# A static instruction order remade from other durations, in a chunked attention with two fp32 layers behind it

## The chip, the cores and the metric

One core of a Trainium2 chip runs the whole program in one launch. The metric is the time of one execution on the device in microseconds, the median of 3 runs. The engines are PE (TensorE), DVE (VectorE), ACT (ScalarE), POOL (GpSimd) and SP (SyncE, which issues the DMAs here).

## The reference

```
attention, q, k, v of (4, 8, 576, 64), in chunks of 64 rows:
    scores = q_c @ k_c.T / 8;  attn = softmax(scores);  out = attn @ v_c
x = out as (2304, 512)
layer 1:  h = x @ w_in (512 x 2048);   g = s * relu(h)**2 + b;   y = g @ w_out (2048 x 512)
layer 2:  h = y @ w_in';               g = softplus(h);          z = g @ w_out'
```

## The kernel before

The tokens are taken as 18 tiles of 128 (two tiles make a unit, three units a group of N = 384 columns, so there are three groups j). Everything is fp32. A product of two fp32 matrices is made of three fp32r matmuls: each operand is split into a high part, which ACT writes as a cast (L505), and a low part, which DVE writes as the difference (L514); high*high, high*low and low*high are added up in PSUM.

**Attention** (tiles t = 0 to 17). For each tile: PE makes the scores (L733), DVE takes the row maximum (L747). For the first six tiles DVE scales the maximum (L769) and ACT makes eight exponentials with their sums (L757); for the others DVE subtracts (L779), ACT takes the exponential (L792) and DVE adds up (L800). DVE forms the reciprocal (L810, L811), POOL multiplies by it (L817), PE transposes (L833), ACT or DVE copies the result out of PSUM (L350 or L352), PE multiplies by the values (L852). Three PSUM buffers, named at, hold scores, transposed tiles and results in turn.

**First product of a layer.** It runs over 24 quads: a quad is 2 by 2 blocks of 128 rows of w_in for one group, made with seven products (L916) in place of eight. The forms that these need (sums and differences of quarters of x and of the weights) are made beforehand: on x by `odd_forms`, `forms`, and on the weights by `weights1`, with DVE and POOL sharing the additions (both record at L492). Inside a quad, products 6, 7 and 5 are chained through PSUM by copies on ACT (L938 and L350/L352) and by differences on DVE (L492); the finished blocks leave through ACT (L948).

**Second product.** In layer 1 six blocks of 16 steps (L1093) read the hidden features back from DRAM, square and scale them, split them and add up in four PSUM buffers. In layer 2 seven products by three groups of eight steps (L1244) do the same with sums that DVE and POOL formed. The weights arrive as 64-bit floats and are turned into fp32 by `convert` (L400 to L472, five instructions on DVE and one on ACT).

**What sets the order.** Nothing is ordered by hand. Each piece of work is recorded as an `Op` with the engines that may run it and a duration on each, a key (the due time written by its author), its dependencies and the buffers that it takes. `Work.order` then plans: again and again it takes the engine whose next piece can start first, among the pieces that can start within 0.02 us of that the one with the lowest key, and gives it its start, its end and its buffers. The list sorted by start is emitted once, so each engine's instructions stand in that order, and each engine works them off in turn: an instruction that waits holds up all behind it. The planned times are used for nothing else; what runs on the chip is the order and the choice of engine and buffer. The durations come from the small functions `dve`, `act`, `pool` and `mm`, and between two pieces on different engines the planner puts a fixed delay:

```
SAME, OTHER, LOAD = 0.13, 0.15762, 2.0
def dve(n, fast=False, pointers=0): return (144 + n / (1.6 if fast else 1)) / 960 + 0.14 * pointers
def act(n, psum=False, pointers=0): return 0.155 + n * 0.00085 + (0 if psum else 0.035) + 0.1 * pointers
def pool(n): return 0.55 + n * 0.0015
```

Of the kernel before, what the change touches and what calls it, by code (L numbers as in the profile page):

```python
# [21 lines left out]
DM = H * D  # L22
DFF = 2048
KK = DM // P
# [9 lines left out]
N = GROUP * P  # L34
# [62 lines left out]

class Work:
# [6 lines left out]
    SAME, OTHER, LOAD = 0.13, 0.15762, 2.0  # L105
# [24 lines left out]
    def order(self, places):  # L130
        free = {k: {i: 0.0 for i in range(n)} for k, n in places.items()}
        engine = {"PE": 0.0, "ACT": 0.0, "DVE": 0.0, "SP": 0.0, "POOL": 0.0}
        memory = 0.0
# [25 lines left out]
        while len(done) < len(self.ops):  # L159
# [10 lines left out]
            t, op, e = best  # L170
# [9 lines left out]
            engine[e] = t + cost  # L180
            op.end = t + cost
# [3 lines left out]
            for u in op.gives:  # L185
                u.left -= 1
                u.until = max(getattr(u, "until", 0.0), op.end)
                if u.left == 0:
                    free[u.kind][u.index] = u.until + self.OTHER
# [26 lines left out]
def block_attention_two_layers(  # L216
# [271 lines left out]
    def sub(key, out, x, y, n, deps, uses=(), op=None, e="DVE", **kw):  # L488
        return add(
            {e: pool(n) if e == "POOL" else dve(n)},  # L490
            key,
            lambda e: on(e).tensor_tensor(  # L492
                out=out(), in0=x(), in1=y(), op=op or ALU.subtract
            ),
            deps,
            uses,
            **kw,
        )

    def split(key, hi, lo, x, n, deps, uses=(), psum=False, r=(), wh=(), wl=()):  # L500
# [11 lines left out]
            {"DVE": dve(n)},  # L512
# [98 lines left out]
    def odd_forms(ph, u, even, odd, key, deps, uses):  # L611
# [18 lines left out]
        o1 = sub(key, x(0), lo(odd), lo(even), 256, deps, uses, after=turn.get("T", ()))  # L630
# [62 lines left out]
    def attention(t, key):  # L693
# [34 lines left out]
        def scores(e):  # L728
# [16 lines left out]
            {"DVE": dve(DM)},  # L745
# [29 lines left out]
        else:  # L775
            o3 = add(
                {"DVE": dve(DM)},
# [20 lines left out]
                {"DVE": dve(DM)},  # L798
# [9 lines left out]
        def reciprocals(e):  # L808
# [6 lines left out]
            {"POOL": pool(DM)},  # L815
# [14 lines left out]
        def turned(e):  # L830
# [7 lines left out]
            {"ACT": act(DM, True), "DVE": dve(DM)},  # L838
# [21 lines left out]
        if hold or not odd:  # L860
            xo = Place("xo")
            c = add(
                {"ACT": act(DM, True), "DVE": dve(DM)},
                key,
                lambda e: copy(e, at(xo), at(px)),
                [o10],
                [px, xo],
            )
            held[t] = xo, c
# [25 lines left out]
    def quad(ph, i, j, w, keys, kinds):  # L895
# [66 lines left out]
        def kept(n, go, o, key):  # L962
# [8 lines left out]
            {"ACT": act(N, True), "DVE": dve(N)},  # L971
# [7 lines left out]
        d7 = sub(keys[5] - 1, lambda: at(dd), acc(ba), lambda: at(s2), N, [p7], [ba, s2, dd])  # L979
        p5 = product(5, ba, [sc, d7])  # L980
        sd = sub(keys[3] - 1, acc(bd), acc(ba), lambda: at(dd), N, [p5], [ba, dd, bd])
# [28 lines left out]
    def block(ph, j, half, t0, first):  # L1010
# [3 lines left out]
        accs = [Place(x) for x in kinds]  # L1014
        gl = None
        for m in range(NM):
# [69 lines left out]
            for d in range(4):  # L1086

                def go(e, d=d, m=m, hi=hi, lo=lo, w2=w2):
# [19 lines left out]
                )  # L1108
                if m == NM - 1:
# [3 lines left out]
                        {"ACT": act(N, True), "DVE": dve(N)},  # L1113
# [28 lines left out]
    def second_by_blocks(ph, t0):  # L1142
# [69 lines left out]
        for z, (n, j) in enumerate(steps):  # L1212
            accs = [Place(x) for x in (("S", "at"), ("S", "at"), ("S", "at"), ("A", "A"))[z % 4]]
            wp, apart = v2[n]
            for i in range(NF):
# [21 lines left out]
                def go(e, i=i, hi=hi, lo=lo, wp=wp, apart=apart, accs=accs):  # L1237
# [18 lines left out]
                    [*parts, *v2_ready[n, i]],  # L1256
# [14 lines left out]
            for d in range(2):  # L1271
                for y, (to, of) in enumerate(plan):
                    dst = (ysum[j] + (to * 2 + d) * N, N)
                    ps = lambda d=d, accs=accs: at(accs[d])[:, :N]
                    if of is None:
                        f = add(
                            {"ACT": act(N, True), "DVE": dve(N)},
# [6 lines left out]
                    else:  # L1284
# [9 lines left out]
                            ALU.add,  # L1294
                            r=[src],
# [177 lines left out]
```

## Time and profile before

| | |
|---|---|
| median of 3 runs | 832.77 us (832.23 to 833.54) |
| span of the profiled execution | 834.3 us |
| PE busy | 795.1 us (95%) |
| weight loads on PE | 775.0 us (93%) |
| DVE busy | 654.0 us (78%) |
| ACT busy | 506.4 us (61%) |
| POOL busy | 148.6 us (18%) |
| mean granted TensorE clock | 0.992 |

The profiled execution is one execution; its span is 1.5 us above the median of the timed runs. PE's idle time is not spread evenly: the slices of the span show it in the first eighth, around 480 us and at the very end. A busy PE is not PE at its peak, since a slow clock and waits inside a row of matmuls count as busy too, so the number of matmuls in a window says more than its busy share.

### The profile page before, as it was taken

The page shows a single profiled execution, that of the slowest core. Times are in us where ns is not written, and L with a number is a line of the kernel's source. Part 1 is how long each engine was busy: PE and PEld are TensorE (multiplying, and loading weights), DVE is VectorE, ACT ScalarE, POOL GpSimd, SP SyncE. Part 2 cuts the span into 40 slices and gives each one's busy share as a digit, 9 for nine tenths or more (in the row PEclk, how much of TensorE's full clock was granted, in tenths as well). Part 3 has the DMA queues.
Part 4 walks back from the last instruction along what each step waited for, and adds up shares of the span by engine and source line. Part 5 has one row for each costly group of instructions (what it writes and reads, how often), then busy time and mean ns, then how long its engine had stood idle before and what let it go on. Part 6 is the DMA issues. An engine that isn't in the chain of part 4 may idle for free.

```text
span 834.3 us, 14524 instructions
## 1 busy us (share of the span) xinstructions
PE 795.1 (95%) x5117; PEld 775.0 (93%) x5117; DVE 654.0 (78%) x1174; ACT 506.4 (61%) x1076; POOL 148.6 (18%) x162
## 2 busy tenths in 40 slices
PE   4688889999999999999999989999999999999998
PEld 3577789999998999999999989999999999999997
DVE  5799888888967869888888776778784767777865
ACT  3655555666656877767767655555555655555543
POOL 4254240111111003222213540111110000000000
PEclk9899999999999999999999999999999999999999
DMA  8665347868757835767662027657667996688851
GB/s 235 195 190 170 106 144 241 262 240 269 257 218 275 324 107 161 244 225 255 224 197 88 11 95 262 232 197 251 246 233 253 354 372 226 203 262 297 277 187 57
DMA packets 80632, 180.26 MB, mean 216 GB/s; under 512 B 9008, under 2 KB 53040, under 8 KB 79664
## 3 DMA queue, kind: packets, MB, share of 16 engines
q1 hardware_dynamic: 80560, 179.34, 63.9%
q8 instruction: 40, 0.66, 0.3%
q14 instruction: 32, 0.26, 0.1%
HBM read 111.15 MB, written 68.16 MB: 215 GB/s over the span
## 4 chain that ended last, share of the span: by engine, by line
PE 83%; DVE 8%; DMA 3%; ACT 3%; issue 1%; POOL 1%; SPq 0%; ACTq 0%; DVEq 0%
PE at L916 17%; PE S L916 10%; PE S L1093 9%; PE at L1093 9%; PE S L1244 8%; PE at L1244 8%; PE A L916 7%; PE A L1093 6%; PE A L1244 5%; DVE operands L514 2%; DVE mem L492 2%; PE at L852 2%; PE at L733 1%; DMA mem<-in_w_dram 1%; DMA last<-in_k_dram 1%
## 5 line engine op out<-in xcount | busy, mean ns | idle before, releaser
L492 POOL TENSOR_TENSOR mem<-mem 128x256 f32<-128x256 f32 x120 | 109.6, 923 | 414.1 <-DVE mem L472 309.2
L514 DVE TENSOR_TENSOR operands<-mem,operands 128x384 fp32r<-128x384 f32 (+4 forms) x186 | 130.9, 720 | 45.0 <-ACT operands L505 43.1
L505 ACT CAST operands<-mem 128x384 fp32r<-128x384 f32 (+4 forms) x186 | 112.3, 620 | 58.8 <-PE at L1244 36.1
L514 DVE TENSOR_TENSOR operands<-last,operands 128x384 fp32r<-128x384 f32 (+2 forms) x184 | 110.5, 616 | 42.4 <-ACT operands L505 39.9
L505 ACT CAST operands<-last 128x384 fp32r<-128x384 f32 (+2 forms) x184 | 94.3, 528 | 73.2 <-PE A L1093 46.5
L916 PE MATMUL at<-operands 128*128 128x384 f32 x624 | 122.4, 340 | 4.1 <-ACT mem L350 2.0
L916 PEld LDWEIGHTS at<-operands 128*128 128x128 f32 x624 | 110.4, 190 | 6.7 <-ACT mem L350 2.7
L1093 PE MATMUL S<-operands 128*128 128x384 f32 x432 | 90.7, 335 | 0.4 <-DVE operands L514 0.4
L1093 PE MATMUL at<-operands 128*128 128x384 f32 x432 | 90.3, 334 | 0.0
L1244 PE MATMUL S<-operands 128*128 128x384 f32 x384 | 87.4, 334 | 0.1
L1244 PE MATMUL at<-operands 128*128 128x384 f32 x384 | 87.1, 334 | 0.0
L916 PE MATMUL S<-operands 128*128 128x384 f32 x420 | 83.5, 337 | 0.9 <-DVE S L492 0.8
L1093 PEld LDWEIGHTS S<-operands 128*128 128x128 f32 x432 | 76.2, 188 | 0.9 <-DVE operands L514 0.6
L1093 PEld LDWEIGHTS at<-operands 128*128 128x128 f32 x432 | 76.2, 188 | 0.0
L948 ACT ACTIVATE mem<-S 128x384 f32<-128x384 f32 x104 | 50.6, 492 | 41.1 <-PE S L916 34.4
L916 PEld LDWEIGHTS S<-operands 128*128 128x128 f32 x420 | 73.5, 188 | 1.5 <-DVE S L492 1.3
L1244 PEld LDWEIGHTS S<-operands 128*128 128x128 f32 x384 | 68.3, 188 | 0.4 <-DVE operands L514 0.4
L1244 PEld LDWEIGHTS at<-operands 128*128 128x128 f32 x384 | 68.3, 188 | 0.0
L916 PE MATMUL at<-last,operands 128*128 128x384 f32 x336 | 67.2, 337 | 0.6 <-ACT S L938 0.2
L492 DVE TENSOR_TENSOR mem<-mem 128x384 f32<-128x384 f32 (+1 forms) x108 | 60.7, 589 | 9.1 <-ACT mem L948 7.8
L1093 PE MATMUL A<-operands 128*128 128x384 f32 x288 | 65.4, 334 | 0.0
L916 PE MATMUL A<-operands 128*128 128x384 f32 x300 | 60.5, 341 | 3.3 <-ACT S L938 1.5
(79 smaller groups left out, 1217.0 us busy)
## 6 DMA issues: line engine op xcount, KB each, us to landing
mem<-in_w_dram SPq DMA_DIRECT2D x64, 512.0 KB, 4.4
summed<-mem SPq DMA_DIRECT2D x168, 192.0 KB, 2.3
mem<-summed SPq DMA_DIRECT2D x30, 768.0 KB, 4.8
hid<-mem SPq DMA_DIRECT2D x96, 192.0 KB, 2.9
last<-hid SPq DMA_DIRECT2D x24, 768.0 KB, 5.3
last<-summed SPq DMA_DIRECT2D x12, 768.0 KB, 4.9
mem<-forms SPq DMA_DIRECT2D x7, 1024.0 KB, 7.1
last<-in_q_dram SPq DMA_DIRECT2D x18, 256.0 KB, 4.2
```

What stands on the lines that cost most here:

```text
L492: lambda e: on(e).tensor_tensor(out=out(), in0=x(), in1=y(), op=op or ALU.subtract),
L505: lambda e: nc.scalar.copy(out=hi().bitcast(F32R), in_=x()),
L514: lambda e: nc.vector.tensor_tensor(out=lo().bitcast(F32R), in0=x(), in1=hi(), op=ALU.subtract),
L733: nc.tensor.matmul(out_[c * D : (c + 1) * D, pr], of("q")[:, pr * P + c * D : pr * P + (c + 1) * D], kb[:, :, pr, c, :], start=True, stop= ...
L852: nc.tensor.matmul(at(px)[y, x], of("v")[y, x], of("aT")[y, x], start=True, stop=True)
L916: nc.tensor.matmul(acc(dst)().rearrange("p (u c) -> p u c", u=GROUP), l[a], r[c], start=start and kk == 0 and x == 0, stop=kk == 1 and x == 2,
L948: lambda e: nc.scalar.activation(out=at(go), in_=acc(place)(), func=AF.Softplus if ph else AF.Relu),
L1093: nc.tensor.matmul(at(accs[d])[:, :N], l[a], r[c], start=m == 0 and z == 0, stop=m == NM - 1 and z == 2,)
L1244: nc.tensor.matmul(at(accs[d])[:, :N], l[a], r[c], start=i == 0 and y == 0, stop=i == NF - 1 and y == 2,)
```

## The change

Only the planner's numbers change, and with them the order, the choice between ACT and DVE for some copies, and the PSUM buffers. No operation is added or removed: the same 3777 pieces are recorded with the same keys.

1. The delay between dependent pieces depends on the engine that ends (`AFTER`) and the one that begins (`BEFORE`), and now also holds on the same engine, other than PE.
2. DVE, ACT and POOL get other durations. On DVE a piece of n elements now takes 0.068 + n/960 us in place of 0.15 + n/960, on POOL 256 elements take 0.683 us in place of 0.934.
3. A duration can be a `Port`: pieces of DVE and POOL that are marked so may not overlap in the plan. DVE pieces that read PSUM, and sums along a row, are not marked.
4. In the blocks and in layer 2's second product each step now depends on the step before it, so that the plan can't exchange them.

```diff
+class Port(float):
+    pass
...
-    SAME, OTHER, LOAD = 0.13, 0.15762, 2.0
+    AFTER = {"PE": 0.225, "ACT": 0.133, "DVE": 0.116, "POOL": 0.078, "SP": 0.0}
+    BEFORE = {"PE": 0.02, "ACT": 0.0, "DVE": 0.0, "POOL": 0.12, "SP": 0.1}
+    HELD = {"DVE": 0.06, "POOL": 0.1}
+    LOAD = 2.0
...
         def earliest(op, e):
-            t = engine[e]
+            t = max(engine[e], port) if isinstance(op.engines[e], Port) else engine[e]
             for d in op.deps:
-                t = max(t, d.end + (self.OTHER if d.on != e else 0 if e == "PE" else self.SAME))
+                t = max(t, d.end + (self.AFTER[d.on] + self.BEFORE[e] if d.on != e or e != "PE" else 0))
...
             engine[e] = t + cost
+            if isinstance(op.engines[e], Port):
+                port = t + cost - self.HELD[e]
...
-def dve(n, fast=False, pointers=0):
-    return (144 + n / (1.6 if fast else 1)) / 960 + 0.14 * pointers
+def dve(n, fast=False, pointers=0, port=True):
+    t = 0.068 + n / 960 / (1.94 if fast else 1) + 0.058 * pointers
+    return Port(t) if port else t
 def act(n, psum=False, pointers=0):
-    return 0.155 + n * 0.00085 + (0 if psum else 0.035) + 0.1 * pointers
+    return 0.09 + n * 0.00083 - (0.035 if psum else 0) + 0.095 * pointers
-def pool(n):
-    return 0.55 + n * 0.0015
+def pool(n, spread=False):
+    return Port(0.135 + n * (0.0017 if spread else 0.00214))
...
-                    [*parts, *w2_done[ph, m]],
+                    [*parts, *w2_done[ph, m], *before[d]],
...
-                    [*parts, *v2_ready[n, i]],
+                    [*parts, *v2_ready[n, i], *([o] if i else [])],
```

**What stands where.** In the new program the line numbers of the old one are higher by 10 up to the quads (L733 is L743, L505 is L515) and by 13 at the end. On PE, about a fifth of the 942 pieces stand at another place; on DVE and ACT nearly all do, most by a few places. 74 pieces change between ACT and DVE: DVE has 1150 pieces in place of 1154, ACT 988 in place of 984. POOL keeps its 150, SP its 547.

The first place is PE at the start of the attention. In the names, at_70, at_71 and at_72 are the three PSUM buffers, and last_120 holds the tiles' inputs. Scores (L733) are of tiles 3, 4, 5 and 6 in turn, transposed tiles (L833) and values (L852) of tiles 1, 2 and 3. Before:

```order
L733 MATMUL at_71<-last_120 64x128 x8
L733 MATMUL at_70<-last_120 64x128 x8
L833 MATMUL at_72<-ident,last_120 128x128 x4
L852 MATMUL at_72<-last_120 64x64 x16
L833 MATMUL at_71<-ident,last_120 128x128 x4
L852 MATMUL at_71<-last_120 64x64 x16
L733 MATMUL at_72<-last_120 64x128 x8
L733 MATMUL at_70<-last_120 64x128 x8
L833 MATMUL at_71<-ident,last_120 128x128 x4
L852 MATMUL at_71<-last_120 64x64 x16
```

Now, from the same place on:

```order
L743 MATMUL at_71<-last_120 64x128 x8
L843 MATMUL at_70<-ident,last_120 128x128 x4
L862 MATMUL at_70<-last_120 64x64 x16
L743 MATMUL at_72<-last_120 64x128 x8
L843 MATMUL at_71<-ident,last_120 128x128 x4
L743 MATMUL at_70<-last_120 64x128 x8
L862 MATMUL at_71<-last_120 64x64 x16
L843 MATMUL at_72<-ident,last_120 128x128 x4
L743 MATMUL at_71<-last_120 64x128 x8
L862 MATMUL at_72<-last_120 64x64 x16
```

Tile 1 is transposed ahead of tile 4's scores, and tile 3 ahead of tile 6's scores and into at_72, which tile 4's scores held, where before it went into at_71, which the result of tile 2 held.

The second place is DVE at the same time: from the copy of the transposed tile 2 (L352, into last_120) to the copy of tile 3. L400, L430 and L444 turn the second weights into fp32; L514 with operands<-at_71 is the split of tile 2's result, which sets its PSUM buffer free. Before:

```order
L352 COPY last_120<-at_71 128x512
L810 TENSOR_SCALAR sm_83<-sm_83 128x8
...
L400 TENSOR_SCALAR mem<-mem 128x512
L430 TENSOR_SCALAR mem<-mem 128x512
L352 COPY mem<-at_71 128x512
...
L747 TENSOR_REDUCE mx_78<-at_72 128x8
L514 TENSOR_TENSOR operands<-mem,operands 128x1024
L514 TENSOR_TENSOR operands<-at_71,operands 128x512
L769 TENSOR_SCALAR mx_78<-mx_78 128x8
L747 TENSOR_REDUCE mx_80<-at_70 128x8
L352 COPY last_120<-at_71 128x512
```

Now, from the same weights on:

```order
L410 TENSOR_SCALAR mem<-mem 128x512
L440 TENSOR_SCALAR mem<-mem 128x512
...
L820 TENSOR_SCALAR sm_83<-sm_83 128x8
...
L362 COPY last_120<-at_71 128x512
L757 TENSOR_REDUCE mx_78<-at_70 128x8
L524 TENSOR_TENSOR operands<-mem,operands 128x1024
L362 COPY mem<-at_71 128x512
L779 TENSOR_SCALAR mx_78<-mx_78 128x8
...
L454 SCALAR_TENSOR_TENSOR mem<-mem 128x512
L524 TENSOR_TENSOR operands<-at_71,operands 128x512
L362 COPY last_120<-at_72 128x512
```

The weights' first instruction now stands ahead of the copy of tile 2 and of tile 3's reciprocal; the maximum of tile 6 no longer stands ahead of the copy of tile 3. On SP the two loads of these weights (in_w_dram) now stand ahead of the three loads of tile 7's q and k, and behind those of tile 6; before they stood behind tile 7's.

The third place is ACT early in layer 2, some 490 us into the span. L505 with last<-mem and 512 elements is a split of the forms of group 2; the first of them in each list needs no sum of POOL's, the second does. L350 is the copy that product 7 of a quad of group 1 waits for. Before:

```order
L505 CAST last_4635<-mem 128x512
L938 COPY S_68<-at_72 128x384
L948 ACTIVATE mem<-S_67 128x384
L948 ACTIVATE mem<-at_71 128x384
L505 CAST last_4635<-mem 128x512
L948 ACTIVATE mem<-S_69 128x384
L350 COPY mem<-at_72 128x384
L938 COPY S_67<-at_70 128x384
L505 CAST last_4635<-mem 128x512
```

Now:

```order
L948 COPY S_69<-at_71 128x384
L515 CAST last_4644<-mem 128x512
L958 ACTIVATE mem<-S_68 128x384
L948 COPY S_67<-at_70 128x384
L360 COPY mem<-at_71 128x384
L515 CAST last_4644<-mem 128x512
L958 ACTIVATE mem<-A_66 128x384
```

In the new list the copy stands ahead of the split that needs POOL's sum; before it stood behind it.

## Rows read from the trace of the kernel before

**Rows 1.** The page: span, busy time by engine, PE's busy tenths in 40 slices.

```profile
span 834.3 us, 14524 instructions
PE 795.1 (95%) x5117; PEld 775.0 (93%) x5117; DVE 654.0 (78%) x1174; ACT 506.4 (61%) x1076; POOL 148.6 (18%) x162
...
PE   4688889999999999999999989999999999999998
```

**Rows 2.** Busy time by window: stretch, length, engines (instructions), granted clock, DMA.

```profile
0.00:20.00 20.00, 9.47 (x57) 7.01 (x57) 11.73 (x22) 8.05 (x36) 8.36 (x17) 1.00 0.88 236
20.00:40.00 20.00, 12.84 (x172) 10.91 (x172) 13.81 (x30) 11.89 (x60) 5.61 (x6) 0.88 0.67 205
40.00:60.00 20.00, 17.04 (x268) 14.36 (x267) 18.23 (x38) 11.86 (x30) 9.44 (x10) 0.86 0.61 182
60.00:80.00 20.00, 17.44 (x270) 15.26 (x271) 19.50 (x39) 12.12 (x21) 7.99 (x10) 1.00 0.61 187
80.00:100.00 20.00, 17.51 (x252) 15.23 (x248) 17.10 (x32) 9.89 (x19) 8.31 (x8) 1.00 0.21 71
...
700.00:750.00 50.00, 50.00 (x291) 50.00 (x290) 37.90 (x71) 28.82 (x57) 0.00 (x0) 1.00 0.72 243
```

**Rows 3.** Timeline of PE, 12 to 47: start, duration, line, [idle before <-releaser].

```profile
32.57 1.15 PE L852 MATMUL at<-last 64*64 64x64 f32 x32 [1.27 <-DVE last L352]
...
39.15 1.09 PE L833 MATMUL at<-ident,last 128*128 128x128 f32 x4 [3.53 <-DVE mx L769]
41.02 1.97 PE L852 MATMUL at<-last 64*64 64x64 f32 x32 [0.78 <-DVE last L352]
```

**Rows 4.** Timeline of ACT, 15 to 47.

```profile
15.80 0.83 ACT L505 CAST operands<-mem 128x768 fp32r<-128x768 f32 x1 [3.87 <-DVE mem L472]
16.54 0.31 ACT L757 ACTIVATE last<-at,mx 128x64 f32<-128x64 f32 x1
```

**Rows 5.** Timeline of DVE, 22 to 47.

```profile
33.81 1.03 DVE L400 TENSOR_SCALAR mem<-mem 128x512 uint32<-128x512 uint32 x1 [0.47 <-DMA mem<-in_w_dram]
...
38.32 0.68 DVE L514 TENSOR_TENSOR operands<-at,operands 128x512 fp32r<-128x512 f32 x1
38.92 0.15 DVE L769 TENSOR_SCALAR mx<-mx 128x8 f32<-128x8 f32 x1
...
45.79 0.69 DVE L747 TENSOR_REDUCE mx<-at 128x8 f32<-128x512 f32 x1 [0.32 <-PE at L733]
```

**Rows 6.** The chain that ended last, 24 to 47: start, duration, what.

```profile
25.67 0.45 SPq L367
...
27.36 6.43 DMA mem<-in_w_dram
```

**Rows 7.** Timeline of DVE, 258 to 272.

```profile
265.76 0.56 DVE L492 TENSOR_TENSOR mem<-at,mem 128x384 f32<-128x384 f32 x1 [0.44 <-PE at L916]
```

**Rows 8.** Timeline of PE, 262 to 273.

```profile
266.93 1.32 PE L916 MATMUL at<-operands 128*128 128x384 f32 x6 [1.20 <-ACT S L938]
```

**Rows 9.** Timeline of PE, 484 to 498.

```profile
488.74 1.20 PE L916 MATMUL S<-operands 128*128 128x384 f32 x6
491.90 3.71 PE L916 MATMUL at<-operands 128*128 128x384 f32 x12 [1.96 <-ACT mem L350]
```

**Rows 10.** Timeline of ACT, 484 to 498.

```profile
490.47 0.62 ACT L505 CAST last<-mem 128x512 fp32r<-128x512 f32 x1 [2.56 <-POOL mem L492]
...
491.38 0.47 ACT L350 COPY mem<-at 128x384 f32<-128x384 f32 x1
```

**Rows 11.** Timeline of POOL, 470 to 497.

```profile
486.23 4.21 POOL L492 TENSOR_TENSOR mem<-mem 128x256 f32<-128x256 f32 x2 [5.38 <-ACT last L505]
...
494.64 1.43 POOL L492 TENSOR_TENSOR mem<-mem 128x256 f32<-128x256 f32 x2 [0.42 <-DVE mem L492]
```

**Rows 12.** Timeline of PE, 672 to 682.

```profile
679.83 0.44 PE L1244 MATMUL A<-operands 128*128 128x384 f32 x1 [0.46 <-ACT operands L505]
680.49 1.83 PE L1244 MATMUL A<-operands 128*128 128x384 f32 x9 [0.21 <-DVE operands L514]
```

More of the change, by code (lines that the diff above doesn't have):

```diff
@@ L132, in order @@
         engine = {"PE": 0.0, "ACT": 0.0, "DVE": 0.0, "SP": 0.0, "POOL": 0.0}
-        memory = 0.0
+        memory = port = 0.0
         users, waits = {}, {}
@@ L186, in order @@
                 u.left -= 1
-                u.until = max(getattr(u, "until", 0.0), op.end)
+                u.until = max(getattr(u, "until", 0.0), op.end + self.AFTER[e])
                 if u.left == 0:
-                    free[u.kind][u.index] = u.until + self.OTHER
+                    free[u.kind][u.index] = u.until
             done.append(op)
@@ L486, in on, with sub @@
         return nc.gpsimd if e == "POOL" else nc.vector
-    def sub(key, out, x, y, n, deps, uses=(), op=None, e="DVE", **kw):
+    def sub(key, out, x, y, n, deps, uses=(), op=None, e="DVE", port=True, **kw):
         return add(
-            {e: pool(n) if e == "POOL" else dve(n)},
+            {e: pool(n) if e == "POOL" else dve(n, port=port)},
             key,
@@ L511, in split @@
         o2 = add(
-            {"DVE": dve(n)},
+            {"DVE": dve(n, port=not psum)},
             key,
@@ L629, in odd_forms @@
         uses = [*uses, t]
-        o1 = sub(key, x(0), lo(odd), lo(even), 256, deps, uses, after=turn.get("T", ()))
+        o1 = sub(key, x(0), lo(odd), lo(even), 256, deps, uses, after=turn.get("T", ()), port=False)
         turn["T"] = [o1]
@@ L744, in attention @@
         o2 = add(
-            {"DVE": dve(DM)},
+            {"DVE": dve(DM, port=False)},
             key,
@@ L776, in attention @@
             o3 = add(
-                {"DVE": dve(DM)},
+                {"DVE": dve(DM, port=False)},
                 key,
@@ L797, in attention @@
             o5 = add(
-                {"DVE": dve(DM)},
+                {"DVE": dve(DM, port=False)},
                 key,
@@ L814, in attention @@
         o7 = add(
-            {"POOL": pool(DM)},
+            {"POOL": pool(DM, True)},
             key,
@@ L837, in attention @@
         o9 = add(
-            {"ACT": act(DM, True), "DVE": dve(DM)},
+            {"ACT": act(DM, True), "DVE": dve(DM, port=False)},
             key,
@@ L862, in attention @@
             c = add(
-                {"ACT": act(DM, True), "DVE": dve(DM)},
+                {"ACT": act(DM, True), "DVE": dve(DM, port=False)},
                 key,
@@ L970, in quad @@
         c2 = add(
-            {"ACT": act(N, True), "DVE": dve(N)},
+            {"ACT": act(N, True), "DVE": dve(N, port=False)},
             keys[7] - 1,
@@ L978, in quad @@
         sc = seed(bc, keys[5] - 1, [p7])
-        d7 = sub(keys[5] - 1, lambda: at(dd), acc(ba), lambda: at(s2), N, [p7], [ba, s2, dd])
+        d7 = sub(keys[5] - 1, lambda: at(dd), acc(ba), lambda: at(s2), N, [p7], [ba, s2, dd], port=False)
         p5 = product(5, ba, [sc, d7])
-        sd = sub(keys[3] - 1, acc(bd), acc(ba), lambda: at(dd), N, [p5], [ba, dd, bd])
+        sd = sub(keys[3] - 1, acc(bd), acc(ba), lambda: at(dd), N, [p5], [ba, dd, bd], port=False)
         b22 = hidden(ba, 1, 1, keys[5] + 1, [p5])
@@ L1014, in block @@
         accs = [Place(x) for x in kinds]
+        before = [[] for d in range(KK)]
         gl = None
@@ L1108, in block @@
                 )
+                before[d] = [o]
                 if m == NM - 1:
@@ L1112, in block @@
                     f = add(
-                        {"ACT": act(N, True), "DVE": dve(N)},
+                        {"ACT": act(N, True), "DVE": dve(N, port=False)},
                         key + dt,
@@ L1276, in second_by_blocks @@
                         f = add(
-                            {"ACT": act(N, True), "DVE": dve(N)},
+                            {"ACT": act(N, True), "DVE": dve(N, port=False)},
                             t,
@@ L1294, in second_by_blocks @@
                             ALU.add,
+                            port=False,
                             r=[src],
```

## The prediction, made before the changed kernel was timed

> **What bounds the kernel now.** Read the page first: PE is busy for 795.1 of 834.3 us, and its tenths are below 8 only in the first two slices [rows 1]. Next, the busy time by window [rows 2]. In a stretch without waits, 700 to 750, PE ends 291 matmuls in 50.00 us, 0.172 us each. The second and first products are 24 x 7 x 6 matmuls per layer, 6 x 16 x 4 x 3 and 21 x 8 x 6 of them, 4176 in all, so 718 us at that rate; no order of the same work goes below this plus the attention's own matmuls. The rest, 116 us, holds those and PE's waits, and only the waits can be won. In the first 100 us PE is busy for 9.47 + 12.84 + 17.04 + 17.44 + 17.51 = 74.3 us, so it waits for 25.7 and, at a granted clock of 0.88 and 0.86 between 20 and 60, works part of the rest at the lower of its two levels. DVE in the same windows goes from 11.73 and 13.81 to 18.23, 19.50 and 17.10: up to 40 us DVE waits too, from 40 on it is full, with 60 - 54.8 = 5.2 us to spare. So the attention has two halves: a start in which every engine waits for another (a latency bound), and a main part that DVE bounds. After 100 the waits are small and show in the tenths as one 8 around 480 [rows 1]. Last, the timelines around the larger gaps of PE, to see which wait ends last there [rows 3 to 12].
>
> **The change part by part.** The recorded pieces are the same; what moves is order, engine and buffer. Chaining the accumulations adds no instruction, and on PE, which takes its work in turn, no wait: nothing. Of the 74 pieces that change engine, DVE loses 4 net, some 0.55 us each, 2 us of 654 spread over the span: nothing on the path by itself.
>
> *The start, -3.0 us.* Three links move. First, tile 1's exponentials start at 16.54 behind a cast that began at 15.80 [rows 4]; in the new list they stand ahead of it, 0.7 us earlier, and tile 1's reciprocal and copy move forward with them. Second, the second weights: SP issues their load at 27.36, after three loads for tile 7 that begin at 25.67, and it lands 6.43 us later [rows 6]; DVE stands before it, and its conversion runs at 33.81 [rows 5]. Now the load is issued 27.36 - 25.67 = 1.7 us earlier, so it lands by 32.1, earlier if tile 7's bytes were what slowed it. Third, PE transposes tile 3 at 39.15 after 3.53 us without work [rows 3]: it waits for a PSUM buffer that DVE's split of tile 2's result sets free, at 38.32 + 0.68 [rows 5]. In the new list it takes the buffer of tile 4's scores, free once ACT has made tile 4's exponentials, which need nothing of tile 2's result. What then binds is DVE's copy of tile 3. Between the copies of tiles 2 and 3 stand, in the new list, one difference 1024 wide, four instructions 512 wide and three small ones. One of 512 takes 0.68 us, and the next starts 0.60 after it [rows 5]; with twice that for 1024 and 0.4 for the small ones, 4.0 us. The copy of tile 2 ended just ahead of its reader, 32.57 [rows 3], and stands now about where it stood, so from 33 the 4.0 us give 37.0. Before, the copy ended just ahead of its reader at 41.02 [rows 3] and so began near 40.3: 3.3 us earlier. Following the two lists on to the maximum of tile 7, the same place in both (45.79 [rows 5]), the lead stays about 3. From there DVE is full; to the end of the attention its work in the two lists differs by under 1 us, so a lead at 45 is a lead at 95, and PE's later work starts that much sooner. Bounds: 0 if the lead is used up, -4.8 if the lower clock [rows 2] also ends sooner; on the other side +1.7, since the weights' first instruction on DVE now stands ahead of tile 2's copy, and if the load lands as late as before, the earlier issue turns into that much waiting of DVE. I take -3.0, near the copy's 3.3.
>
> *The end of layer 1's first product, -1.0 us.* Product 5 of the last quad starts at 266.93 after 1.20 us [rows 8]; it waits for DVE's difference at 265.76 [rows 7], which stood behind the splits of layer 2's first weights. These splits now stand several places further ahead, and PE has product 2 between 7 and 5. What is late next: the first block's low part, five DVE instructions behind the last quad's, as before. Bounds -1.4 and +0.6.
>
> *The second layer's entry, -2.4 us.* PE ends product 6 at 488.74 + 1.20 = 489.94 and starts product 7 at 491.90, 1.96 us later [rows 9], waiting for a copy that ACT makes at 491.38, behind a cast that waited 2.56 us for POOL and ran at 490.47 [rows 10]. In the new list the copy stands ahead of that cast, and PE has another quad's product 3 in between: the 1.96 go. The twelve matmuls from 491.90 took 3.71 where 12 x 0.172 plus the last one's tail of 0.16 make 2.2 [rows 9]; a third of these 1.5 us should go too, as ACT is no longer late. POOL's pair of sums at 486.23 takes 4.21 us against 1.43 for an equal pair at 494.64 [rows 11]: DVE has instructions without a pause beside it. The new list has one DVE instruction fewer there, which wins 0.5 for POOL; since nothing urgent waits behind it now, I count nothing. Bounds -3.6 and +1.0 (a POOL sum that becomes the wait of PE itself).
>
> The Trainium skill, page "SBUF — State Buffer", section "SBUF: two separate sides", says that the pair of ports is locked for one whole instruction, by whichever of the two engines starts first. By that rule the pair at 486.23 would have waited for one DVE instruction, 0.68 us, and taken 0.68 + 1.43 = 2.1 us; the trace shows 4.21, so here a waiting POOL is passed over by several DVE instructions, and the plan, which gives POOL the port after one, is too kind to it. By the rule this entry could win the whole 3.5 us, in place of the 2.4.
>
> *The start of layer 2's second product, -0.9 us.* At 679.83 and 680.49 PE waits 0.46 and 0.21 us [rows 12], each time behind the 0.16 that the last matmul takes over its 0.172, so 1.0 in all, at the change to the A buffers, because ACT and DVE make their copies of a finished result before the splits that PE needs next. In the new lists the splits stand first. Bounds -1.1 and +0.5.
>
> *Everything else, +1.0 us.* Elsewhere after 100 us PE's gaps are small ones, behind seeds and differences inside the quads. The new order has others. That it is planned with durations nearer to the rows (0.60 us from one 512 wide DVE instruction to the next, where the old plan had 0.68 [rows 5]) speaks for fewer; that the due times are as they were, and POOL slower than planned, for more. Bounds -1.5 and +4. I take +1.0, the size of one gap such as that of [rows 8].
>
> Sum: -3.0 - 1.0 - 2.4 - 0.9 + 1.0 = -6.3. The profiled execution goes from 834.3 to 828.0. The median before, 832.77, lies 1.5 us under that span; taken off alike, the forecast is 826.5 us.
>
> **The rivals.**
>
> *POOL is starved in the attention (slower).* The lead makes DVE run without a pause earlier, and the softmax multiplication (L817) on POOL is on every tile's chain. Against 1.43, the pair of [rows 11] took 2.8 us more. For it: DVE has 19.50 of 20 us between 60 and 80 [rows 2]. Against it: in that window POOL already works 7.99 us beside that DVE, and once DVE has nothing left but what waits for POOL, POOL gets its turn. From three such multiplications on the path on, the sum turns: 3 x 2.8 = 8.4 against 6.3, so +2.1, or 834.9.
>
> *Only the transitions are won.* The lead at 45 is eaten in the main part, since PE's order there is fixed too and a tile that stands ahead of one that is ready makes it wait; ten waits of half a DVE instruction (0.3 us) are the 3.0. For it: the main part has little room to catch up [rows 2]; against it: both lists are full there. -6.3 + 3.0 = -3.3, or 829.5.
>
> *The change does not do what it says.* The order is better in the plan, but each engine's queue on the chip waits at other places, and new gaps take back what the named ones give: everything else at +4, the lead at half, -1.5, the entry at -1.5, the other two as they are, -1.9, in all -0.9, or 831.9. That is within 0.2% (1.7 us), about what a measurement of this kernel can tell from no change. For it: the due times are those of the old durations; against it: the named gaps rest on one instruction's place each.
>
> *All of it and more.* The lead with the clock, -4.8, the entry at -3.6, the other two at -2.0 and nothing new: -10.4, or 822.4.
>
> **How the numbers follow.** The forecast has 0.45, the larger gain 0.14, the transitions alone 0.17, no change 0.10, starved POOL 0.14. Faster by over 0.2%: 0.45 + 0.14 + 0.17, and a little of the neighbours' spread, 0.77; within 0.2%: 0.10; slower: 0.13. The forecast's own range is 824 to 829.2. The range that should hold 8 in 10 goes down to 821.5, below the larger gain, and up to 833.0, past no change, and leaves out starved POOL and the far ends.
>
> **What would show it.** In the changed profile, tile 3 is transposed (L843) by about 36 and not 39, with little idle before it; the second weights' load lands by 32; the maximum of tile 7 runs at about 43; DVE is no less full from 40 to 95. The gaps of PE at 266.93, 491.90 and 679.83, each some us earlier now, are under 0.4. It is wrong if L817 takes longer in the mean than before; if DVE has more idle time between 45 and 95 than the 5 us now; or if PE has new gaps of over 1 us between 100 and 660.

## The result, and the profile after

| | before | after |
|---|---|---|
| median | 832.96 us (832.23 to 833.54, 4 runs) | 818.35 us (816.57 to 819.81, 4 runs) |
| ratio of the medians, 95% interval | | 0.9825 (0.9804 to 0.9846) |
| span of the profiled execution | 834.3 us | 816.4 us |

The change makes the kernel 14.6 us faster by the medians. The prediction had the direction; its 826.5 us and its lower end of 821.5 us were too high. The two profiled spans differ by 17.9 us: the execution of before that was profiled was slower than its timed runs (span 834.3, where their median less the 1.8 us around the span that the later runs show, as 818.22 us for the span of 816.4, makes 831.2).

The page after, answering to [rows 1]:

```profile
span 816.4 us, 14526 instructions
...
PE 788.6 (97%) x5117; PEld 771.9 (95%) x5117; DVE 637.4 (78%) x1170; ACT 507.4 (62%) x1080; POOL 144.7 (18%) x162
...
PE   5788999999999999999999999999999999999998
```

PE reaches 9 tenths in the fifth slice, before in the seventh, and the 8 around 480 us is gone. DVE is busy for 16.6 us less with four instructions less: the reader should stop there, since four instructions of 0.55 us are only 2.2.

The windows, answering to [rows 2] (same columns):

```profile
20.00:40.00 20.00, 14.17 (x190) 11.66 (x188) 14.89 (x35) 14.00 (x72) 6.04 (x7) 0.74 0.67 195
40.00:60.00 20.00, 17.21 (x278) 14.86 (x275) 19.55 (x39) 11.42 (x19) 8.21 (x10) 1.00 0.72 200
...
80.00:100.00 20.00, 19.50 (x244) 17.91 (x243) 17.31 (x33) 16.14 (x32) 10.25 (x10) 1.00 0.37 123
...
700.00:750.00 50.00, 50.00 (x291) 50.00 (x290) 36.98 (x71) 28.26 (x56) 0.00 (x0) 1.00 0.77 253
```

The stretch without waits is as before, 291 matmuls in 50 us. From 80 to 100 PE is busy for 19.50 us where it was 17.51. From 40 to 60 its granted clock is 1.00 where it was 0.86, but from 20 to 40 it is 0.74 where it was 0.88; over the first 50 us the mean is 0.90 in both.

At the start, PE, DVE and the chain, answering to [rows 3, 5, 6]:

```profile
32.23 1.11 PE L843 MATMUL at<-ident,last 128*128 128x128 f32 x4
34.63 1.98 PE L743 MATMUL at<-last 128*64 128x128 f32 x16 [1.29 <-DVE operands L524]
...
36.54 1.59 PE L862 MATMUL at<-last 64*64 64x64 f32 x32
```

```profile
28.30 0.43 DVE L410 TENSOR_SCALAR mem<-mem 128x512 uint32<-128x512 uint32 x1 [0.98 <-DMA mem<-in_w_dram]
...
40.50 0.68 DVE L757 TENSOR_REDUCE mx<-at 128x8 f32<-128x512 f32 x1
```

```profile
21.78 6.50 DMA mem<-in_w_dram
```

Tile 3 is transposed at 32.23 without a wait (before 39.15, after 3.53 us of waiting), the weights land at 28.3 (before 33.8), tile 3's values start at 36.54 (before 41.02), and tile 7's maximum runs at 40.50 (before 45.79).

Around the end of layer 1's first product, the second layer's entry and the start of the last product, PE, answering to [rows 8, 9, 12]:

```profile
252.64 1.20 PE L926 MATMUL S<-operands 128*128 128x384 f32 x6
...
258.30 0.45 PE L1104 MATMUL S<-operands 128*128 128x384 f32 x1 [0.85 <-ACT operands L515]
259.06 1.14 PE L1104 MATMUL S<-operands 128*128 128x384 f32 x5 [0.31 <-DVE operands L524]
...
466.47 1.32 PE L926 MATMUL S<-operands 128*128 128x384 f32 x6 [1.39 <-ACT S L948]
...
478.24 1.20 PE L926 MATMUL at<-operands 128*128 128x384 f32 x6
...
662.58 3.63 PE L1256 MATMUL A<-operands 128*128 128x384 f32 x20
```

The 1.20 us ahead of product 5 and the 1.96 ahead of product 7 are gone (478.24 is that product 7), and the change to the A buffers has no gap. The first block now waits 0.85 and 0.31, and the entry has one new gap of 1.39. PE of before ahead of the gap of [rows 8] and at the first block:

```profile
264.52 1.21 PE L916 MATMUL at<-operands 128*128 128x384 f32 x6
...
271.05 1.15 PE L1093 MATMUL S<-operands 128*128 128x384 f32 x5 [0.38 <-DVE operands L514]
```

Where the time came from is read from the same matmul at six places of PE's list. The third column is from the first experiment, a second execution of before's order:

| PE starts | before, us | same order again, us | after, us | after's lead grows by, against the two |
|---|---|---|---|---|
| scores of tile 7 | 43.96 | 43.66 | 38.64 | 5.3 / 5.0 |
| product 7 of quad (2, 0), layer 1 | 139.80 | 140.66 | 129.22 | 5.3 / 6.4 |
| a step of the first block | 280.37 | 281.19 | 268.36 | 1.4 / 1.4 |
| a product after layer 2's entry | 520.56 | 518.80 | 505.18 | 3.4 / 0.8 |
| a step of the last product | 699.15 | 697.31 | 681.30 | 2.5 / 2.4 |
| the last matmuls | 829.15 | 827.31 | 811.30 | 0.0 / 0.0 |

The second line is the surprise: 5 to 6 us between 40 and 140 us, where the prediction had a kept lead.

### The profile page after: what moved, and what is told of

Its sections match the earlier page's. It is cut to its first block, busy times and chain, and to the rows that moved or that the text cites. A ratio compares the mean times of both kernels' runs of the same rounds, so it can differ in the third digit from the quotient of the medians.

```text
span 816.4 us, 14526 instructions
## 1 busy us (share of the span) xinstructions
PE 788.6 (97%) x5117; PEld 771.9 (95%) x5117; DVE 637.4 (78%) x1170; ACT 507.4 (62%) x1080; POOL 144.7 (18%) x162
## 4 chain that ended last, share of the span: by engine, by line
PE 88%; DVE 5%; ACT 2%; DMA 2%; issue 1%; SPq 1%; POOL 0%; DVEq 0%; ACTq 0%; POOLq 0%
PE at L926 19%; PE S L926 12%; PE S L1104 9%; PE at L1104 9%; PE S L1256 8%; PE at L1256 8%; PE A L926 8%; PE A L1104 6%; PE A L1256 5%; PE at L862 1%; DVE operands L524 1%; SPq L377 1%; PE at L743 1%; DVE mem L502 1%; DMA last<-in_k_dram 1%
## 5 line engine op out<-in xcount | busy, mean ns | idle before, releaser
L524 DVE TENSOR_TENSOR operands<-mem,operands 128x384 fp32r<-128x384 f32 (+4 forms) x186 | 126.0, 698 | 53.9 <-ACT operands L515 52.2
L515 ACT CAST operands<-mem 128x384 fp32r<-128x384 f32 (+4 forms) x186 | 111.2, 620 | 59.2 <-PE at L1256 36.2
L515 ACT CAST operands<-last 128x384 fp32r<-128x384 f32 (+2 forms) x184 | 94.4, 527 | 75.7 <-PE A L1104 48.7
```

Of the source, the lines that this page charges most:

```text
L515: lambda e: nc.scalar.copy(out=hi().bitcast(F32R), in_=x()),
L524: lambda e: nc.vector.tensor_tensor(out=lo().bitcast(F32R), in0=x(), in1=hi(), op=ALU.subtract),
```

## The experiments

A ratio is to runs of before from the same set, and need not be the quotient of the medians printed here. Before's median was 832.69 us in the sets of the first four experiments, of POOL's price and of the first moved model, 833.03 where one part is left out, and 833.66 for the last four.

**The same order once more.** Part 4 of the change alone:

```diff
-                    [*parts, *w2_done[ph, m]],
+                    [*parts, *w2_done[ph, m], *before[d]],
```

> The kernel before with part 4 of the change alone: each step of an accumulation depends on the step before it. The planned order of every engine comes out as before, piece by piece, so every theory expects 833.0 us and no difference. The run has a second use. The trace of before shows the first keys landing 1.0 to 1.7 us later than that of after, at places that the change doesn't touch, and its span is some 3 us over what its timed runs imply. If the profiled execution of before had a late start by chance, this profile has a span near 831 and tile 1's scores start at about 11.5 and not 12.46; if the late landing belongs to the order of before, they start at 12.46 again.

Measured: 833.76 us, ratio 1.0005 (0.9976 to 1.0034). Chaining makes no difference that shows. The span is 832.4; tile 1's scores start at 13.82, 1.4 us later than in before, so the landing of the first loads varies by itself; yet tile 7's scores start 0.3 us earlier. The second layer's entry came out otherwise than in before. Of this execution, POOL, DVE and PE, answering to [rows 11] and [rows 9]:

```profile
487.04 2.07 POOL L492 TENSOR_TENSOR mem<-mem 128x256 f32<-128x256 f32 x2 [5.38 <-ACT last L505]
```

```profile
487.29 1.23 DVE L514 TENSOR_TENSOR last<-mem,last 128x512 fp32r<-128x512 f32 x1
488.44 1.09 DVE L492 TENSOR_TENSOR mem<-mem 128x384 f32<-128x384 f32 x1
```

```profile
490.59 2.36 PE L916 MATMUL at<-operands 128*128 128x384 f32 x12
```

DVE of before at the same two instructions:

```profile
486.47 0.68 DVE L514 TENSOR_TENSOR last<-mem,last 128x512 fp32r<-128x512 f32 x1
487.07 0.55 DVE L492 TENSOR_TENSOR mem<-mem 128x384 f32<-128x384 f32 x1
```

In before the pair of sums took 4.21 us while DVE ran on undisturbed; here, in the same order, POOL got in, the pair took 2.07, DVE paid with 1.23 and 1.09, and product 7 has no wait ahead of it and takes 2.36 in place of 3.71. So 2.6 us of the entry in before was the outcome of one execution.

**Where the time is won.** Three kernels plan with the new numbers only in one part of the plan's own time (45 us: `now < 45`; 130 us: `now < 130`; the complement: `now >= 130`):

```diff
+            new = now < 45
...
+            if not new:
+                cost = getattr(cost, "old", None) or cost
```

> The new numbers (durations, delays and port) while the plan's own time is under 45 us, the old numbers from there on. Theory A (the gain of 14.6 us is won in three or four separate places: about 3 at the start to 45 us, 5 between 85 and 111 us where the first quads of layer 1 meet the last tiles of the attention, 3.4 at the second layer's entry, 1.6 at its second product, 1 to 2 elsewhere): 829 to 830 us, that is the start alone. Theory B (it is nearly all an earlier start, which is passed on, and the later gaps only close because everything comes sooner): 820 to 822.

> The new numbers while the plan's own time is under 130 us, so in the whole attention and in the first quads, the old numbers from there on. Theory A (separate places): the start and the handover are won, the second layer's entry and second product are not: 833 - 3 - 5 = 825 us. Theory B (an earlier start passed on): 820 to 822, and no less than the run with 45 us.

> The old numbers while the plan's own time is under 130 us, the new numbers from there on: the complement of the run before. Theory A: 14.6 - 8 = 6 to 7 us are won after the attention, 826 to 827 us. Theory B: nothing to win there beyond 1 or 2 us, 831 to 832.

Measured: up to 45, 827.15 us, ratio 0.9939 (0.9912 to 0.9966); up to 130, 823.85, 0.9901 (0.9870 to 0.9931); from 130 on, 829.53, 0.9962 (0.9940 to 0.9984). Theory B is out: its 820 to 822 us for the first two came out in neither. Theory A, separate places, holds in kind: 8.8 and 3.2 us make 12.0 of the 14.6. Its sizes hold only for the second kernel (825 expected); the first won 2 to 3 us more than its 829 to 830, and the third 3 us less than its 826 to 827, so 2.6 us belong to neither half, no more than the intervals can hide. In the trace of the first one a lead of 2.8 us at tile 7's scores (41.12 for 43.96) has shrunk to 1.0 at the product 7 that before starts at 139.80: a lead is not kept by itself. That execution took 831.33 us, 4.2 over the kernel's median, so the loss need not be as large in the others.

**Which part wins it.** The changed kernel without one part each, without the port (part 3), with the old delays (part 1), with the old durations (part 2):

```diff
-            t = max(engine[e], port) if isinstance(op.engines[e], Port) else engine[e]
+            t = max(engine[e], port) if False else engine[e]
```

```diff
-                t = max(t, d.end + (self.AFTER[d.on] + self.BEFORE[e] if d.on != e or e != "PE" else 0))
+                t = max(t, d.end + (0.15762 if d.on != e else 0 if e == "PE" else 0.13))
```

```diff
-    return Port(0.135 + n * (0.0017 if spread else 0.00214))
+    return Port(0.55 + n * 0.0015)
...
-    t = 0.068 + n / 960 / (1.94 if fast else 1) + 0.058 * pointers
+    t = (144 + n / (1.6 if fast else 1)) / 960 + 0.14 * pointers
```

> The changed kernel without its part 3: pieces of DVE and POOL may overlap in the plan, everything else new. The runs so far won 5.5 us with the new numbers up to 45 us of the plan, 8.8 up to 130 and 3.2 from 130 on, 14.6 in all, and the traces show DVE taking 3 us less for the same conversions of the first weights between 45 and 90, because fewer of them run beside an instruction of POOL. Theory P (what counts is that the plan keeps DVE and POOL apart, so that DVE's instructions are not stretched): most of the 14.6 goes, 826 to 830 us, and L444's conversions beside POOL take 1.3 to 1.6 again and not 0.68. Theory D (what counts are the shorter durations, which put each piece nearer to where the chip has it): 818 to 821 us.

> The changed kernel without its part 1: the old delays between pieces (0.13 on the same engine, 0.158 to another), new durations and port. Theory P (port): 818 to 821 us. Theory D (durations): 818 to 821. Theory W (the delays count, since DVE's and POOL's results reach another engine sooner than the old plan thought and PE's later, 0.116 + 0.02 and 0.245 in place of 0.158): 825 to 829.

> The changed kernel without its part 2: the old durations of DVE, ACT and POOL, with the new delays and the port. With the long durations the port costs the plan far more than the chip. Theory P: 820 to 824 us. Theory D: 828 to 834, the same as before or slower, since a plan that thinks POOL's pieces take 0.93 and holds DVE back for them makes DVE the bound where it is not.

Measured: without the port 842.40 us, ratio 1.0130 (1.0101 to 1.0159), slower than before; with the old delays 829.57, 0.9959 (0.9938 to 0.9980); with the old durations 835.39, 1.0035 (1.0014 to 1.0055). The port was expected to cost at most 12 and cost 24. One place of many in that trace, a block of layer 1 with a weights' conversion, all engines:

```profile
406.31 2.74 POOL L502 TENSOR_TENSOR mem<-mem 128x256 f32<-128x256 f32 x3 [2.82 <-DVE mem L482]
406.62 0.96 DVE L410 TENSOR_SCALAR mem<-mem 128x512 uint32<-128x512 uint32 x1
...
407.50 0.96 DVE L440 TENSOR_SCALAR mem<-mem 128x512 uint32<-128x512 uint32 x1
...
408.49 1.11 DVE L454 SCALAR_TENSOR_TENSOR mem<-mem 128x512 f32<-128x512 uint32 x1
...
409.53 0.55 DVE L524 TENSOR_TENSOR operands<-last,operands 128x384 fp32r<-128x384 f32 x1
...
410.13 1.16 PE L1104 MATMUL S<-operands 128*128 128x384 f32 x5 [0.99 <-DVE operands L524]
```

Three conversions beside POOL's sums take 0.96, 0.96 and 1.11; the split behind them comes late and PE waits 0.99 us. In the blocks of the changed kernel PE has no such wait (its lead is 12.01 us at 280 and at 467 alike), and its conversions on DVE stand clear of POOL:

```profile
394.42 0.68 DVE L454 SCALAR_TENSOR_TENSOR mem<-mem 128x512 f32<-128x512 uint32 x1
...
395.42 0.69 DVE L482 SCALAR_TENSOR_TENSOR mem<-mem 128x512 f32<-128x512 f32 x1
```

The kernel with old durations still has 6.4 us of lead at 268, as theory P wants, and loses 4.7 of it where PE turns to the first block (its wait there is 3.27 us); its time as a whole lies just above theory D's range.

**POOL's price by itself.** Three orders, as they are, with POOL's instructions made small:

```diff
-                out=out(), in0=x(), in1=y(), op=op or ALU.subtract
+                out=less(e, out()), in0=less(e, x()), in1=less(e, y()), op=op or ALU.subtract
...
-                out=heads(of("e")),
+                out=heads(of("e"))[:, :, :4],
```

> The kernel before with its order as it is, but each instruction of POOL made small: the sums take 16 of 256 columns, the softmax multiplication 4 of 64 per head (the rest of those values is left out; two fills of the buffers concerned stand on DVE before the first scores). POOL then occupies nothing for long. Theory P (the order of before loses its time where DVE and POOL meet): 818 to 823 us, near the changed kernel's 818.35. Theory O (it loses it because pieces stand in the wrong places, whatever they take): 829 to 833.

> The order that was planned without the port (842.4 us), with POOL's instructions made small in the same way. Theory P: the plan without the port is right about a chip on which POOL takes nothing from DVE, so the time falls to 812 to 820 us, by more than 22. Theory O: 835 to 840.

> The changed kernel with POOL's instructions made small in the same way. Theory P: its order already keeps the two engines apart, so little is left to win: 813 to 817 us. Theory O: the same 2 to 5 us as the other two.

Measured, and what POOL costs each order (the medians' difference to the same order with POOL's full work; ratios are to before):

| order | POOL full | POOL small, ratio | POOL costs |
|---|---|---|---|
| before | 832.69 us | 822.50 us, 0.9889 (0.9824 to 0.9953) | 10.2 us |
| planned without the port | 842.40 us | 823.86 us, 0.9885 (0.9828 to 0.9942) | 18.5 us |
| after | 818.35 us | 817.04 us, 0.9814 (0.9762 to 0.9867) | 1.3 us |

The full and the small kernel of the last two orders were timed in different sets; by the ratios POOL costs 9.2, 20.4 and 0.9 us, so the last is not told from nothing. Theory P holds in direction for all three and in size for the first; the last, at 817.04, lies at the edge of its 813 to 817, and the middle one fell by 18.5 and not by over 22. Theory O's 829 to 833 and 835 to 840 came out in neither of the first two. But POOL's price is not all: with POOL small in both, the order after is still 5.5 us faster than the order before (817.04 against 822.50). POOL's price thus explains 8 to 9 of the 14.6 us, and other places the rest. The trace of before with POOL small shows which: read at the same matmuls it leads before by 2.0 us at tile 7's scores, 7.5 at product 7 of layer 1, 12.8 behind layer 2's entry and 13.3 at the end, where the changed kernel leads by 5.3, 10.6, 15.4 and 17.9. From 44 to 140 both win some 5.4; 3.3 us of the start and 2 of the last product are not had by making POOL small.

One rival is left in these runs. A small POOL instruction also ends sooner itself (a sum takes 0.34 us in the mean and not 0.92), so what "POOL costs" holds waits for POOL's results as well as DVE's lengthened work, and no run separates the two. In the traces ACT's waits that end with POOL are 7.1 us in before, 8.4 in after and 17.3 in the plan without the port, and at most 1.5 with POOL small. Between 44 and 140 us of before, PE's waits that end with POOL come to 0.9 us and those that end with DVE to 5.8 (3.5 with POOL small), and DVE's busy time up to the transposition of tile 17 falls from 78.3 to 73.6: there DVE's lengthened work is the larger part.

What the meeting of the two engines does in the order of before, where the last tiles of the attention meet the first quads: DVE, POOL and PE of before,

```profile
85.98 1.56 DVE L458 SCALAR_TENSOR_TENSOR mem<-mem 128x512 uint32<-128x512 uint32 x1
...
90.86 1.29 DVE L444 SCALAR_TENSOR_TENSOR mem<-mem 128x512 f32<-128x512 uint32 x1
...
94.18 2.04 DVE L492 TENSOR_TENSOR mem<-mem 128x256 f32<-128x256 f32 x2
96.14 1.48 DVE L514 TENSOR_TENSOR operands<-mem,operands 128x768 fp32r<-128x768 f32 x1
97.54 0.54 DVE L492 TENSOR_TENSOR mem<-A,mem 128x384 f32<-128x384 f32 x1
```

```profile
85.94 1.05 POOL L817 TENSOR_TENSOR last<-last,sm 128x512 f32<-128x512 f32 x1 [2.57 <-DVE sm L811]
90.55 1.05 POOL L817 TENSOR_TENSOR last<-last,sm 128x512 f32<-128x512 f32 x1 [3.56 <-DVE sm L811]
...
94.71 1.23 POOL L817 TENSOR_TENSOR last<-last,sm 128x512 f32<-128x512 f32 x1
95.90 2.30 POOL L492 TENSOR_TENSOR mem<-mem 128x256 f32<-128x256 f32 x2
```

```profile
98.14 1.31 PE L916 MATMUL A<-operands 128*128 128x384 f32 x6 [1.49 <-DVE mem L492]
```

and the same instructions of the same order with POOL small, DVE and PE:

```profile
83.33 0.76 DVE L458 SCALAR_TENSOR_TENSOR mem<-mem 128x512 uint32<-128x512 uint32 x1
...
88.20 0.68 DVE L444 SCALAR_TENSOR_TENSOR mem<-mem 128x512 f32<-128x512 uint32 x1
...
90.91 0.78 DVE L497 TENSOR_TENSOR mem<-mem 128x256 f32<-128x256 f32 x2
91.74 0.96 DVE L519 TENSOR_TENSOR operands<-mem,operands 128x768 fp32r<-128x768 f32 x1
92.62 0.55 DVE L497 TENSOR_TENSOR mem<-A,mem 128x384 f32<-128x384 f32 x1
```

```profile
93.22 1.34 PE L921 MATMUL A<-operands 128*128 128x384 f32 x6 [0.18 <-DVE mem L497]
```

The four groups take 6.37 us beside POOL and 3.18 without, the difference that PE waits for comes at 97.54 and 92.62, and PE's wait falls from 1.49 to 0.18. The changed kernel reaches the same at PE by order, with POOL's work in full:

```profile
83.66 0.56 DVE L502 TENSOR_TENSOR mem<-A,mem 128x384 f32<-128x384 f32 x1
...
84.54 0.68 DVE L468 SCALAR_TENSOR_TENSOR mem<-mem 128x512 uint32<-128x512 uint32 x1
...
85.73 0.68 DVE L454 SCALAR_TENSOR_TENSOR mem<-mem 128x512 f32<-128x512 uint32 x1
...
87.20 1.27 DVE L502 TENSOR_TENSOR mem<-mem 128x256 f32<-128x256 f32 x1
88.50 1.40 DVE L524 TENSOR_TENSOR operands<-mem,operands 128x768 fp32r<-128x768 f32 x1
```

```profile
88.22 1.32 PE L926 MATMUL A<-operands 128*128 128x384 f32 x6
```

The difference stands ahead of the conversions, these run at 0.68, and product 5 has no wait. The sum and the split behind them are still lengthened (1.27 and 1.40): the two engines meet here too, but PE does not wait for it.

**Luck or cause.** The changed kernel with its model moved a little:

```diff
-    t = 0.068 + n / 960 / (1.94 if fast else 1) + 0.058 * pointers
+    t = 0.075 + n / 960 / (1.94 if fast else 1) + 0.058 * pointers
...
-    return Port(0.135 + n * (0.0017 if spread else 0.00214))
+    return Port(0.15 + n * (0.0017 if spread else 0.00214))
```

> The changed kernel with its model moved a little: 0.075 in place of 0.068 as DVE's constant, 0.15 in place of 0.135 as POOL's. A greedy plan turns this into another order (some 100 of PE's 942 pieces stand elsewhere, most of DVE's). Theory P: the time stays within 816 to 822 us. Theory L (the gain of the change is the luck of one order among many): anywhere between 815 and 842.

Measured: 823.39 us, ratio 0.9874 (0.9818 to 0.9931), 5.0 us over the change, outside theory P's range and far from the upper end of L's. Then the same two constants in the plan without the port and in the plan with the old delays, and the port's release times set to 0 (`HELD = {"DVE": 0.0, "POOL": 0.0}`):

> The plan without the port, with the two constants moved as in the jitter of the changed kernel (0.075 and 0.15). If the port is the cause, 836 us or more again, over every plan that has it; if luck, it lies among the others, 818 to 832.

> The plan with the old delays, new durations and the port, with the two constants moved in the same way. If the delays are a cause of their own, 827 us or more again; if the 829.6 was luck, 817 to 825.

> The changed kernel with the port held to the very end of a piece (HELD 0.06 and 0.1 both 0). Theory P with a few us of luck: 818 to 824 us. If the release times decide: over 826.

Measured: without the port 849.46 us, ratio 1.0203 (1.0171 to 1.0235): the port is a cause, +24 and +26 us. With the old delays 822.18, 0.9862 (0.9828 to 0.9897): by one pair of plans the old delays cost 11 us, by the other they win 1, so an effect of the delays of their own is not shown, and the 829.57 lies within the luck of an order. With the release times at 0, 831.59, 0.9983 (0.9964 to 1.0003): this came out as the theory that they decide, but it is one plan. Its lead on before is 2.1 us at tile 7's scores in place of 5.3 and 1.7 at product 7 of layer 1 in place of 10.6; whether release time or luck did it stays open.

**Other keys.**

```diff
-START = [28.0, 40.0, 56.0, 64.0, 84.0, 92.0, 100.0]
-W_KEY = [1.0, 45.0]
+START = [25.9, 40.0, 56.0, 63.8, 85.8, 87.9, 106.5]
+W_KEY = [0.0, 42.2]
```

> The changed kernel's model with other keys: quads 4 to 7 of the list start 0.2 to 6.5 us earlier or later, the first weights' keys 1 and 2.8 earlier, the later weights 3 us later, tiles 2.62 apart in place of 2.5. In the plan this is 2 us better. If the plan holds on the chip to that size: 815 to 818 us; since another order is 5 us of luck, anything between 813 and 824 is no surprise.

Measured: 823.78 us, ratio 0.9893 (0.9863 to 0.9923). What is 2 us better in the plan is 5 worse on the chip. None of the kernels with POOL's full work beats the change.

## Why the prediction was wrong in size

**The start, -3.0, was 5.3** (5.0 against the second execution). The steps are all in the trace: no wait ahead of tile 3's transposition, the earlier load, the maximum of tile 7. The load was sized by its places on SP alone (1.7 us); it was issued 5.6 earlier (21.78 for 27.36), since what SP waited for came earlier too. Tile 3's values start 4.5 earlier (36.54 for 41.02 [rows 3]), where I had 3.3. The lower clock came and went earlier as well, and tile 3's values took 1.59 in place of 1.97, but its share of the first 50 us is the same (mean 0.90 in both), and the second execution of before's order, with a mean of 0.76 there, starts tile 7's scores 0.3 us earlier. So it is not shown that the clock turned the 3.0 into 5.3, as my bound of -4.8 has it; what did so beside the earlier load stays open.

**"From there DVE is full; to the end of the attention its work in the two lists differs by under 1 us, so a lead at 45 is a lead at 95": this step failed.** I counted DVE's work by instructions of fixed length. Up to the transposition of tile 17 both lists have the same 20 conversions of the first weights; their durations add up to 15.1 us before and 12.0 after, and DVE is busy for 78.3 and 74.3 us up to there. PE transposes tile 17 at 96.00 and 89.38. The lead grew by 5 to 6 us on to 140, where I had 0 and some share of "everything else". The view that I left out was DVE's timeline between 85 and 98, with instructions at twice their length beside POOL. I looked at [rows 11], the one place where POOL lost to DVE, made of it a rival in which POOL starves, and never asked what DVE loses to POOL. With POOL's work small, DVE is busy for 616.1 us in the order of before and 611.1 in that of after, so POOL lengthens DVE's work by 38 us before (654.0) and 26 after (637.4).

**"Everything else, +1.0"** had the wrong sign. Beside the 5 to 6 us above, small gaps between 140 and 260 and between 540 and 640 went as well, 1.3 and 0.8 us. The argument that held it up, "POOL slower than planned, for more", was half of the new model: what the port is for, DVE beside POOL, stood in the diff, and its price had rows in the trace. One of my signs of being wrong did come, a new gap of over 1 us (1.39 at 466.47); the rival in which POOL starves did not, since its multiplication takes 1.09 us in the mean and took 1.10.

**The end of the first product, -1.0, was 0.1.** The 1.4 us from 140 to the first block are not it: the matmuls of equal rank ahead of the gap start at 264.52 and 252.64, a lead of 11.9 already, and the first block's second row at 271.05 and 259.06, a lead of 12.0. The named gap of 1.20 is gone, but the first block waits for 0.85 and 0.31 in place of 0.38. So what was late next, which I had "as before", took back nearly all of the gain. **The last product's start, -0.9, was 1.6.**

**The entry, -2.4, was 3.4 against the profiled execution and 0.8 against the second one of the same order.** The reading of the queue was right (the copy stands ahead of the cast that waits for POOL, 478.24 has no gap), but the price rested on one outcome of a contest that goes either way. Its mean over the two executions is 2.1.

**The skill's rule** on the pair of ports explains half. The Trainium skill, page "SBUF — State Buffer", section "SBUF: two separate sides", lets whichever engine starts first hold the pair for one instruction. Where POOL is first, the traces agree: POOL's 85.94 + 1.05 and 90.55 + 1.05 end at 86.99 and 91.60, and DVE's instruction, begun in between, ends 0.55 us later each time (85.98 + 1.56 = 87.54, 90.86 + 1.29 = 92.15). Where DVE is first they differ: POOL waits behind one instruction in one execution and behind several in the other. I used the rule against the change and not on the rows where it speaks for it.

**Of the 14.6 us about 10 are the model's and some 4 this order's luck.** That is an estimate: two neighbours of the change, at 823.39 and 823.78 us, win 9 to 10. It rests on few plans, and the one at 831.59 lies outside. The old model was planned once only, so how lucky or unlucky before's own order is stays open.

## What to carry to other kernels

A duration read from a trace belongs to what ran beside it: list the same instruction's shortest and longest rows, and where they differ by a factor of two, find the engine that it met before costing an order by counts. In an order that a planner makes, a missing conflict can be hidden by padded durations, so that taking the padding away alone makes it slower (842.40 against 833.03 us here); durations and conflicts have to change together. Judge such a change by several plans, and a gap of 2 us by two executions.

## What the runs showed that I had not expected

- One order, two executions: the same pair of sums on POOL takes 4.21 and 2.07 us, and the second layer's entry differs by 2.6 us, with the same instructions in the same queues.
- In these orders it matters less how much DVE is lengthened than where. The plan without the port has 40 us of it (652.1 with POOL in full, 612.2 with POOL small), the order of before 38, and they lose 18.5 and 10.2 us by it; after has 26 and loses about 1.
- Moving two constants of the model by 0.007 and 0.015 us costs 5 us: a greedy plan passes a small difference on to all that follows.
